# Routing logits of a mixture-of-experts kernel with the gate columns as TensorE weights, on four column groups

## The chip, the core and the metric

The kernel runs on one core of one Trainium2 chip. The metric is the device time of one execution in microseconds, the median of several. The profile is that of one execution; its span is what the hardware profiler recorded from the first to the last instruction. Engines are named as in the profile: PE is TensorE's products, PEld its weight loads, DVE VectorE, ACT ScalarE, POOL GpSimd, SP SyncE (which issues most DMAs).

## What is computed

Three layers stand one behind the other. Attention of 4 x 8 heads (576 positions, 64 wide) with a local or a strided mask gives `x` of 2304 tokens x 512. A dense feed-forward layer follows, then a mixture of 8 experts of which each token takes the one with the highest gate logit. The change touches the two products with `w_gate` and `w_output_gate`, 8 columns each.

```python
def _moe_ref(x, w_in, w_out):
    h = x @ w_in
    g = h * np.clip(h + 3.0, 0.0, 6.0) / 6.0
    return g @ w_out

def _moe2_ref(x, w_gate, w_output_gate, w1, w2):
    logits = x @ w_gate
    e_idx = np.argmax(logits, axis=1)
    ...
    eom = 1.0 / (1.0 + np.exp(-(x @ w_output_gate)))
    for e in range(E):
        mask = e_idx == e
        h = np.maximum(x[mask] @ w1[e], 0.0)
        out[mask] = gate_w[mask, None] * eom[mask, e, None] * (h @ w2[e])
```

## The kernel before

**Stages.** The 2304 tokens go in 6 chunks of 384 (three tiles of 128). Attention is cut into 32 groups, 0 to 31; its instructions are spread over the chunks ahead of the one that needs them: chunk 3 needs the groups up to 23, chunk 4 those up to 29, chunk 5 the last two. Behind chunk 5 come the experts (`A` and 1 to 7).

**A chunk's dense layer** has 16 steps f. A step has 12 products `h` (L542, 128x384, two PSUM buffers), ACT's `r` and `gh` (L546, L557), DVE's `r` and `gh` (L552, L564), then 9 products `x2` (L577, 128x512), which add up over f in three PSUM buffers, one for each tile.

**A group of attention** goes: scores `sa`, `sb` (L405, two row groups of 64) on PE; masks and minimum on DVE (L417); exponentials on ACT (L422); sum and reciprocal on DVE (L426, L427); `p` on POOL (L428); transpositions `ta`, `tb` (L452) on PE; their copy `pt` on ACT (L454); `o` (L469, 64-column groups) on PE; `xh` on ACT (L489) and `xl` on DVE (L490), which are the moving operands of `h`. On PE a group's transpositions stand ahead of the next group's scores, and `o` behind these.

**A chunk's routing** stands in the next chunk's first steps. The sums leave PSUM as `x2r` (`r_evac`: L592 on DVE for tiles 0 and 2, L590 on ACT for tile 1; three buffers); `r_trans` transposes them (`xt`, L603) and ACT copies the result to `x2T` (L608, one buffer). `r_logits` multiplies: in four products `x2T`'s 128 columns are the weights and `wgo`'s 16 columns (the two gates side by side) move; the result `lg` (L621) has a token in each partition. fp32 products are recorded as two instructions each. Then come `r_choose` and `r_rank` (`rk`, L651 to L655, weights `ones` and `tri`), and each tile's rows are scattered by POOL (L687) to the expert's place in `xs_d`. `sa`, `lg`, `rk` and `cntp` share one PSUM buffer ("s"); `sb`, `ta` and `xt` share another ("t").

**Chunk 5.** At step 7 `o_first` counts the tokens of each expert (`cntp`, L705); the first expert's number goes through a register to SP, which then issues the loads of its weights (L775) and, from step 10 on, of its rows and their numbers `e_m` (L826). DVE makes `e_i` of `e_m` (L854) and transposes the rows (L832).

**Order.** The code names an order in which work is handed on; within the loop over chunks a list scheduler then sets each engine's order by its own simulated times (attention with a higher priority), so a change in one place may move others. From the end of chunk 5 the order is written by hand.

Of the kernel before, what the change touches and what calls it, by code (L numbers as in the profile page):

```python
# [9 lines left out]
F32 = mybir.dt.float32  # L10
# [4 lines left out]
ACTF = mybir.ActivationFunctionType  # L15
ALU = mybir.AluOpType
AX = mybir.AxisListType
# [5 lines left out]
def kernel(  # L23
# [14 lines left out]
    nc = tc.nc  # L38
# [3 lines left out]
    E, _, DF2 = w1.shape  # L42
    KD = DM // 128
# [3 lines left out]
    NCH = NT // CH  # L47
# [3 lines left out]
    STR = 32  # L51
    NTB = S // STR
    SCL = 1.0 / float(D) ** 0.5
    NEG = -1.0e9 / SCL
    QB = 96
# [10 lines left out]
    const = ctx.enter_context(tc.tile_pool(name="const", bufs=1))  # L66
# [11 lines left out]
    ps_s = ph1.enter_context(tc.tile_pool(name="ps_s", bufs=1, space=PSUM))  # L78
# [4 lines left out]


    ident = const.tile([128, 128], F32, name="ident")
    mask_l0 = const.tile([QB, 128], F32, name="mask_l0")
    mask_l = const.tile([QB, 128], F32, name="mask_l")
    mask_s = const.tile([SB, SB], F32, name="mask_s")
    tri = const.tile([128, 128], F16, name="tri")
    ones = const.tile([128, 128], F16, name="ones")  # L90
    wgo = const.tile([128, KD, 2 * E], F32, name="wgo")
    three = const.tile([128, 1], F32, name="three")
    prio = const.tile([128, E], F32, name="prio")
    tok = const.tile([128, NTILE], F32, name="tok")
# [15 lines left out]

    def consts_attn():
        make_identity(nc, ident)
        for m, b0 in ((mask_l0, 0), (mask_l, STR)):

            nc.gpsimd.memset(m, 0.0)
            nc.gpsimd.affine_select(out=m, in_=m, pattern=[[-1, 128]], base=b0, channel_multiplier=1,
                                    compare_op=ALU.is_ge, fill=NEG)
            nc.gpsimd.affine_select(out=m, in_=m, pattern=[[1, 128]], base=STR - 1 - b0, channel_multiplier=-1,
                                    compare_op=ALU.is_ge, fill=NEG)
        ms = mask_s.rearrange("p (c j) -> p c j", c=CPB)  # L120
        nc.gpsimd.memset(mask_s, 0.0)
        for pat, base, cm in (([[-NTB, CPB], [-1, NTB]], 0, 1), ([[-NTB, CPB], [0, NTB]], 0, 1),
                              ([[NTB, CPB], [0, NTB]], NTB - 1, -1)):
            nc.gpsimd.affine_select(out=ms, in_=ms, pattern=pat, base=base, channel_multiplier=cm,
                                    compare_op=ALU.is_ge, fill=NEG)
        nc.gpsimd.memset(three, 3.0)

    def consts_route():
        nc.gpsimd.memset(tri, 1.0)
        nc.gpsimd.affine_select(out=tri, in_=tri, pattern=[[1, 128]], base=-1, channel_multiplier=-1,  # L130
                                compare_op=ALU.is_ge, fill=0.0)
        nc.gpsimd.iota(prio, pattern=[[-1, E]], base=E, channel_multiplier=0, allow_small_or_imprecise_dtypes=True)
        nc.gpsimd.iota(tok, pattern=[[128, NTILE]], base=-BIG, channel_multiplier=1,
                       allow_small_or_imprecise_dtypes=True)

        nc.gpsimd.memset(base16, 0.0)
        nc.gpsimd.iota(base16[0:1, :], pattern=[[NT, E]], base=0, channel_multiplier=0,
                       allow_small_or_imprecise_dtypes=True)
        nc.gpsimd.iota(eid, pattern=[[1, E]], base=0, channel_multiplier=0, allow_small_or_imprecise_dtypes=True)
        for p in range(E):  # L140
            nc.gpsimd.memset(capc[:, p:p + 1], float(CAPS[p]))
        nc.gpsimd.memset(acc[:, 0, :], 0.0)
        nc.sync.dma_start(out=wgo[:, :, 0:E], in_=w_gate.rearrange("(c p) e -> p c e", p=128))
        nc.sync.dma_start(out=wgo[:, :, E:2 * E], in_=w_ogate.rearrange("(c p) e -> p c e", p=128))

# [92 lines left out]
    def nat(u):  # L238

        return u < 2 * KD  # L240
# [137 lines left out]
    def blk(loc, i):  # L378
        if loc:
            k0 = 0 if i == 0 else QB * i - STR  # L380
            return QB * i, QB, k0, 128
        n = min(SB, S - SB * i)
        return SB * i, n, SB * i, n
# [3 lines left out]
    def banks(n, alt, a, b):  # L387

        pools = {"h": ps_h, "x2": ps_x, "s": ps_s, "t": ps_t}
        return [pools[tag].tile([128, 4, 128], F32, tag=tag, name=f"{nm}{n}") for tag, nm in (a, b)]  # L390

    def at_scores(n, alt=False):
        u, loc, bl = groups[n]
        qt, kt = qk_T["q", u], qk_T["k", u]
        if alt:
            s = banks(n, alt, *((("h", "sa"), ("h", "sb")) if n % 2 else (("s", "sa"), ("x2", "sb"))))
        else:
            s = banks(n, alt, ("s", "sa"), ("t", "sb"))

        with tc.manual_schedule(engines={mybir.EngineType.PE}):  # L400
            for j, i in enumerate(bl):
                q0, qn, k0, kn = blk(loc, i)
                for h2 in (1, 0):
                    p0 = 64 * h2
                    nc.tensor.matmul(s[h2][0:qn, j, 0:kn], lhsT=qt[p0:p0 + 64, q0:q0 + qn],  # L405
                                     rhs=kt[p0:p0 + 64, k0:k0 + kn], start=True, stop=True)
        if nat(u):
            w = w_p.tile([128, 2, 4, 128], F32, tag="w", name=f"p{n}")
            p = [w[:, h2] for h2 in range(2)]
        else:  # L410
            p = [a_p.tile([128, TPC, 128], F32, tag="p", name=f"p{n}_{h2}", bufs=2) for h2 in range(2)]
        st = a_p.tile([128, 2, 3, 4], F32, tag="st", name=f"st{n}", bufs=2)
        for h2 in range(2):
            for j, i in enumerate(bl):
                q0, qn, k0, kn = blk(loc, i)
                m = (mask_l0 if i == 0 else mask_l) if loc else mask_s
                nc.vector.tensor_tensor_reduce(  # L417
                    out=p[h2][0:qn, j, 0:kn], in0=s[h2][0:qn, j, 0:kn], in1=m[0:qn, 0:kn], scale=-SCL, scalar=3.0e38,
                    op0=ALU.add, op1=ALU.min, accum_out=st[0:qn, h2, 0, j:j + 1])
            for j, i in enumerate(bl):  # L420
                q0, qn, k0, kn = blk(loc, i)
                nc.scalar.activation(out=p[h2][0:qn, j, 0:kn], in_=p[h2][0:qn, j, 0:kn], func=ACTF.Exp,  # L422
                                     bias=st[0:qn, h2, 0, j:j + 1], scale=-1.0, accum_out=st[0:qn, h2, 1, j:j + 1])
            for j, c, qn, kn in runs(loc, bl):
                st1, st2 = (st[0:qn, h2, a, j:j + c] for a in (1, 2))
                nc.vector.tensor_scalar(out=st1, in0=st1, scalar1=1e-9, scalar2=None, op0=ALU.add)  # L426
                nc.vector.reciprocal(st2, st1)  # L427
                nc.gpsimd.tensor_tensor(out=p[h2][0:qn, j:j + c, 0:kn], in0=p[h2][0:qn, j:j + c, 0:kn],  # L428
                                        in1=st2.unsqueeze(2).to_broadcast([qn, c, kn]), op=ALU.mult)
        g_p_t[n] = p  # L430

    def runs(loc, bl):

        res = []
        for j, i in enumerate(bl):
            q0, qn, k0, kn = blk(loc, i)
            if res and res[-1][2:] == (qn, kn):
                res[-1] = (res[-1][0], res[-1][1] + 1, qn, kn)
            else:
                res.append((j, 1, qn, kn))  # L440
        return res
# [169 lines left out]
    def r_logits(c, t):  # L611

        if t == 0:
            rt[c] = (r_p.tile([128, 8, TPC, E], F32, tag="rt", name=f"rt{c}", bufs=1),
                     r_p.tile([128, 8, TPC], F32, tag="rm", name=f"rm{c}", bufs=1),
                     r_p.tile([128, TPC, E], F16, tag="oh", name=f"oh{c}", bufs=2),
                     r_p.tile([128, TPC], I32, tag="idx", name=f"idx{c}", bufs=2))
        o = x2T_t.pop((c, t))
        lg = ps_s.tile([128, 2 * E], F32, tag="s", name=f"lg{c}_{t}")
        for kt in range(KD):  # L620
            nc.tensor.matmul(lg, lhsT=o[:, kt, :], rhs=wgo[:, kt, :], start=(kt == 0), stop=(kt == KD - 1))  # L621
        nc.vector.tensor_copy(rt[c][0][:, 0:2, t, :], lg.rearrange("p (a e) -> p a e", a=2))

    def r_choose(c, a, z):
# [374 lines left out]
    for t in range(T0 + 1):  # L999
# [3 lines left out]
        if t == 1:  # L1003
            nc.tensor.matmul(warm[0:96, 0:256], lhsT=g_p_t[t][0][0:96, 0, 0:96],
                             rhs=ident[0:96].unsqueeze(1).to_broadcast([96, 2, 128]), start=True, stop=True)
# [82 lines left out]
    c = NCH - 1  # L1088
# [118 lines left out]
    with tc.If(total > 0):  # L1207
        with ExitStack() as ph3:
# [3 lines left out]
            with tc.For_i(0, E, 1) as e:  # L1212
# [5 lines left out]
                with tc.For_i(0, n_over, 128):  # L1218
# [20 lines left out]
                    for f in range(KF2):  # L1239
                        hp_ = ps_f.tile([128, 128], F32, name="hp_", bufs=2)  # L1240
                        for c in range(KD):
                            nc.tensor.matmul(hp_, lhsT=wr1[:, c, f * 128:(f + 1) * 128], rhs=xt[:, c, :],
                                             start=(c == 0), stop=(c == KD - 1))
                        nc.scalar.activation(out=ht[:, f, :], in_=hp_, func=ACTF.Relu)
                    yp = ps_f.tile([128, DM], F32, name="yp")
                    for f in range(KF2):
# [4 lines left out]
                        out=out, out_offset=bass.IndirectOffsetOnAxis(ap=ids.bitcast(U32), axis=0),  # L1251
                        in_=yr, in_offset=None, bounds_check=NT - 1, oob_is_err=False)
# [30 lines left out]
```

## Time and profile before

| | us |
|---|---|
| median of 3 runs | 867.54 (863.79 to 869.41) |
| profiled execution, its own time | 865.39 |
| its span | 863.6 |
| PE busy | 814.4 (94% of the span) |
| DVE, ACT, POOL busy | 469.7, 400.0, 112.7 |

The page's second part cuts the span into 40 slices of 21.6 us. PE is above 90% in nearly all of them from the ninth on; PEclk, the clock that TensorE was granted in tenths of 2.4 GHz, has a dip in one of them. No other engine reaches 60% over the span. The chain of waits that ended last names only the last scatter of the output, so that stages are read from the windows and from the timeline.

### The profile page before, as it was taken

How to read it: one execution, taken by the hardware profiler on the slowest of the kernel's cores; microseconds unless marked ns; L12 is line 12 of the kernel's file. 1: busy time of each engine (PE TensorE's matmuls, PEld its weight loads, DVE VectorE, ACT ScalarE, POOL GpSimd, SP SyncE). 2: the span in 40 equal slices, each digit the busy share in tenths (PEclk: the TensorE clock that was granted, in tenths of full speed). 3: DMA queues.
4: the chain of work that ended last, by engine and by line, in shares of the span. 5: the costliest groups of instructions: out<-in, count | busy, mean ns of one | idle time of the engine just before them, and what ended most of it. 6: DMA issues, size and time to landing. Idle time of an engine off the chain costs nothing. (4 is left out here: it accounts for less than half of the span.)

```text
span 863.6 us, 14576 instructions
## 1 busy us (share of the span) xinstructions
PE 814.4 (94%) x4928; PEld 692.7 (80%) x4929; DVE 469.7 (54%) x1412; ACT 400.0 (46%) x1054; POOL 112.7 (13%) x191
## 2 busy tenths in 40 slices
PE   7779989599999999999998999999999999999996
PEld 4555545257888888888877899988889999999995
DVE  3687446567764435453454232245656756766671
ACT  3785344467554334444344322334334544555551
POOL 3131003001200102110021010010100011011110
PEclk9669999699999999999997999999999999999999
DMA  3977216973212104320142010044066565657630
GB/s 92 288 218 223 89 51 114 198 171 65 69 34 41 33 9 79 76 42 20 28 109 40 1 39 1 1 134 124 38 190 197 162 183 174 185 180 214 190 127 19
DMA packets 179188, 91.68 MB, mean 106 GB/s; under 512 B 101369, under 2 KB 165113, under 8 KB 179112
## 3 DMA queue, kind: packets, MB, share of 16 engines
q1 hardware_dynamic: 175992, 81.15, 36.8%
q0 software_dynamic: 3120, 9.59, 2.9%
q8 instruction: 39, 0.64, 0.3%
q14 instruction: 37, 0.30, 0.1%
HBM read 74.63 MB, written 16.60 MB: 106 GB/s over the span
## 5 line engine op out<-in xcount | busy, mean ns | idle before, releaser
L577 PE MATMUL x<-wo,gh 128*128 128x512 f32 x720 | 188.3, 398 | 1.1 <-DVE gh L564 0.8
L542 PE MATMUL h<-xh,wi 128*128 128x384 f32 x640 | 182.1, 347 | 2.6 <-ACT xh L489 1.7
L577 PEld LDWEIGHTS x<-wo,gh 128*128 128x128 f32 x720 | 131.5, 188 | 26.5 <-DVE gh L564 2.2
L542 PEld LDWEIGHTS h<-xh,wi 128*128 128x128 f32 x640 | 119.0, 192 | 8.6 <-ACT xh L489 2.0
L546 ACT ACTIVATE r<-h,three 128x384 f32<-128x384 f32 x96 | 55.7, 580 | 133.9 <-PE h L542 76.8
L542 PE MATMUL h<-xl,wi 128*128 128x384 f32 x320 | 110.8, 346 | 0.6 <-DVE xl L490 0.6
L428 POOL TENSOR_TENSOR p<-p,st 126x126 f32<-126x126 f32 (+5 forms) x80 | 61.2, 782 | 366.5 <-DVE st L427 258.1
L552 DVE SCALAR_TENSOR_TENSOR r<-r,h 128x384 f32<-128x384 f32 x80 | 44.2, 552 | 109.0 <-ACT r L546 107.9
L422 ACT ACTIVATE p<-p,st 96x128 f32<-96x128 f32 (+2 forms) x176 | 67.1, 385 | 40.4 <-DVE st L417 40.4
L874 ACT ACTIVATE hh<-eh 128x128 fp32r<-128x128 f32 (+7 forms) x64 | 26.3, 411 | 102.2 <-PE eh L867 97.6
L875 DVE SCALAR_TENSOR_TENSOR hh<-eh,hh 128x128 fp32r<-128x128 f32 (+7 forms) x64 | 29.3, 458 | 74.6 <-ACT hh L874 67.2
L564 DVE TENSOR_TENSOR gh<-r,gh 128x384 fp32r<-128x384 f32 x80 | 46.4, 580 | 42.7 <-ACT gh L557 41.2
L557 ACT ACTIVATE gh<-r 128x384 fp32r<-128x384 f32 x80 | 42.0, 525 | 52.8 <-DVE r L552 43.1
L542 PEld LDWEIGHTS h<-xl,wi 128*128 128x128 f32 x320 | 61.5, 192 | 4.2 <-DVE xl L490 0.9
L572 PE MATMUL x<-wf,gh 128*128 128x512 f32 x96 | 47.2, 628 | 0.0
L538 PE MATMUL h<-x,wf 128*128 128x384 f32 x128 | 46.9, 512 | 0.2 <-DVE wf L215 0.2
L914 POOL DMA_INDIRECT out_dram<-yo,e_i x21 | 21.3, 1015 | 190.9 <-ACT yo L950 169.6
L405 PE MATMUL sb<-kT,qT 64*96 64x128 f32 (+2 forms) x176 | 33.6, 322 | 9.9 <-ACT pt L454 9.3
L538 PEld LDWEIGHTS h<-x,wf 128*128 128x128 f32 x128 | 24.9, 198 | 19.6 <-issue 6.0
L405 PEld LDWEIGHTS sb<-kT,qT 64*96 64x96 f32 (+2 forms) x176 | 24.6, 194 | 19.9 <-ACT pt L454 10.4
L687 POOL DMA_INDIRECT xs_d<-x2r,idx x18 | 19.0, 1054 | 161.8 <-DVE idx L658 110.8
L469 PE MATMUL o<-pt,v 128*64 128x96 f32 (+2 forms) x352 | 31.9, 293 | 2.3 <-ACT wo L221 1.5
(259 smaller groups left out, 1607.4 us busy)
## 6 DMA issues: line engine op xcount, KB each, us to landing
rawi<-in_moe_w_in_dram SPq DMA_DIRECT2D x16, 512.0 KB
rawo<-in_moe_w_out_dram SPq DMA_DIRECT2D x16, 512.0 KB
xs_d<-z SPq DMA_DIRECT2D x8, 792.0 KB
xs<-xs_d SPq DMA_DIRECT2D x28, 128.0 KB
qr<-in_q_dram SPq DMA_DIRECT2D x48, 72.0 KB
kr<-in_k_dram SPq DMA_DIRECT2D x48, 72.0 KB
v<-in_v_dram SPq DMA_DIRECT2D x20, 160.0 KB
er0i<-in_moe_w_dram SPq DMA_DIRECT2D x8, 256.0 KB
```

The costliest lines, as they stand in the source:

```text
L405: nc.tensor.matmul(s[h2][0:qn, j, 0:kn], lhsT=qt[p0:p0 + 64, q0:q0 + qn], rhs=kt[p0:p0 + 64, k0:k0 + kn], start=True, stop=True)
L422: nc.scalar.activation(out=p[h2][0:qn, j, 0:kn], in_=p[h2][0:qn, j, 0:kn], func=ACTF.Exp, bias=st[0:qn, h2, 0, j:j + 1], scale=-1.0, accum ...
L428: nc.gpsimd.tensor_tensor(out=p[h2][0:qn, j:j + c, 0:kn], in0=p[h2][0:qn, j:j + c, 0:kn], in1=st2.unsqueeze(2).to_broadcast([qn, c, kn]), ...
L469: nc.tensor.matmul(o[64 * h2:64 * h2 + 64, q0 - q00:q0 - q00 + qn], lhsT=vt[0:kn, i, :], rhs=pt[h2][0:kn, j, 0:qn], start=True, stop=True)
L538: nc.tensor.matmul(h, lhsT=w_val("i", f)[:, kt * 128:(kt + 1) * 128], rhs=x0[kt // 2][:, kt % 2], start=(kt == 0), stop=(kt == KD - 1))
L542: nc.tensor.matmul(h, lhsT=wa[f][:, a, kt, :], rhs=x[:, kt, c0:c0 + CH], start=(n == 0), stop=(n == 3 * KD - 1))
L546: nc.scalar.activation(out=r, in_=h, func=ACTF.Relu, bias=three, scale=1.0)
L552: nc.vector.scalar_tensor_tensor(out=r, in0=r, scalar=6.0, in1=h, op0=ALU.min, op1=ALU.mult)
L557: nc.scalar.activation(out=gh[:, 0, :], in_=r, func=ACTF.Copy)
L564: nc.vector.tensor_tensor(out=gh[:, 1, :], in0=r, in1=gh[:, 0, :].bitcast(F32), op=ALU.subtract)
L572: nc.tensor.matmul(acc_ps[c][t], lhsT=gh[:, t * 128:(t + 1) * 128], rhs=w_val("o", f), start=(f == 0), stop=(f == KF - 1))
L577: nc.tensor.matmul(acc_ps[c][t], lhsT=gh[:, g, t * 128:(t + 1) * 128], rhs=w[:, a, :], start=(f == 0 and n == 0), stop=(f == KF - 1 and n ...
```

## The change

For chunks 0 to 4 each of the four products of `r_logits` takes 32 columns of `wgo` as weights (16 gates and 16 zeros) and moves the 128 columns of `x2T`; each writes its own 32 partitions of a 128x128 tile `lp` and not one sum. ACT copies `lp` over `x2T`'s first part. One more product, with that copy as weights and a constant `sel_g` (16 columns, each with a one in four rows) moving, adds the four parts and turns them, so that `lg` comes out as before. Chunk 5 keeps the old products. Lines behind L618 move by 14 (`cntp` L705 becomes L719), those between by 3 (L542 becomes L545). The local mask is made once with 160 columns and read at an offset.

```diff
-    wgo = const.tile([128, KD, 2 * E], F32, name="wgo")
+    wgo = const.tile([128, KD, 32], F32, name="wgo")
+    sel_g = const.tile([128, 2 * E], F32, name="sel_g")
...
+        nc.gpsimd.memset(wgo, 0.0)
+        nc.vector.tensor_reduce(out=sel_g, in_=ident.rearrange("p (k e) -> p e k", k=KD)[:, 0:2 * E, :], axis=AX.X,
+                                op=ALU.add)
...
-                m = (mask_l0 if i == 0 else mask_l) if loc else mask_s
+                m = mask_l[:, STR if i == 0 else 0:] if loc else mask_s
...
         o = x2T_t.pop((c, t))
-        lg = ps_s.tile([128, 2 * E], F32, tag="s", name=f"lg{c}_{t}")
-        for kt in range(KD):
-            nc.tensor.matmul(lg, lhsT=o[:, kt, :], rhs=wgo[:, kt, :], start=(kt == 0), stop=(kt == KD - 1))
+        if c < NCH - 1:
+
+            lp = ps_s.tile([128, 128], F32, tag="s", name=f"lp{c}_{t}")
+            with tc.manual_schedule(engines={mybir.EngineType.PE}):
+                for kt in range(KD):
+                    nc.tensor.matmul(lp[32 * kt:32 * kt + 32, :], lhsT=wgo[:, kt, :], rhs=o[:, kt, :], start=True,
+                                     stop=True)
+            nc.scalar.activation(out=o[:, 0, :], in_=lp, func=ACTF.Copy)
+            lg = ps_s.tile([128, 2 * E], F32, tag="s", name=f"lg{c}_{t}")
+            nc.tensor.matmul(lg, lhsT=o[:, 0, :], rhs=sel_g, start=True, stop=True)
+        else:
+            lg = ps_s.tile([128, 2 * E], F32, tag="s", name=f"lg{c}_{t}")
+            for kt in range(KD):
+                nc.tensor.matmul(lg, lhsT=o[:, kt, :], rhs=wgo[:, kt, 0:2 * E], start=(kt == 0), stop=(kt == KD - 1))
```

The scheduler orders the whole program anew. Four places in which it now stands otherwise follow; a name's first numbers are group, or chunk and step (h3_0: chunk 3, step 0) or chunk and tile (x2_2_0).

**PE, from chunk 2 to chunk 3.** Before, behind group 23's output:

```order
L469 MATMUL o23_3584<-pt23_3481,v25_1_0_3268 64x96
L469 MATMUL o23_3584<-pt23_3481,v25_0_0_3133 64x96
L577 MATMUL x2_2_0_2929<-wo15_2618,gh2_15_3797 128x512 x3
L577 MATMUL x2_2_1_2930<-wo15_2618,gh2_15_3797 128x512 x3
L577 MATMUL x2_2_2_2931<-wo15_2618,gh2_15_3797 128x512 x3
L542 MATMUL h3_0_3809<-xh_116,wi0_1878 128x384
L542 MATMUL h3_1_3917<-xh_116,wi1_1896 128x384
```

and now:

```order
L472 MATMUL o23_3615<-pt23_3512,v25_1_0_3299 64x96
L472 MATMUL o23_3615<-pt23_3512,v25_0_0_3158 64x96
L545 MATMUL h3_0_3840<-xh_116,wi0_1873 128x384
L545 MATMUL h3_1_3948<-xh_116,wi1_1891 128x384
L545 MATMUL h3_0_3840<-xl_117,wi0_1873 128x384
```

Chunk 2's last nine `x2` products now stand ahead of group 23's transpositions; behind its output comes at once a product `h3_0` that reads it.

**PE, from chunk 3 to chunk 4.** Before, behind group 28's scores:

```order
L405 MATMUL sa28_4171<-kT12_4058,qT12_4056 96x128
L469 MATMUL o27_4313<-pt27_4152,v15_0_0_3532 64x126
L469 MATMUL o27_4313<-pt27_4152,v15_1_0_3649 64x72
L469 MATMUL o27_4313<-pt27_4152,v15_0_0_3532 64x72
L542 MATMUL h3_13_4671<-xh_116,wi13_2547 128x384
L542 MATMUL h3_13_4671<-xl_117,wi13_2547 128x384
L542 MATMUL h3_13_4671<-xh_116,wi13_2547 128x384 x2
L542 MATMUL h3_13_4671<-xl_117,wi13_2547 128x384
L542 MATMUL h3_13_4671<-xh_116,wi13_2547 128x384
L577 MATMUL x2_3_0_3942<-wo12_2453,gh3_12_4659 128x512 x3
```

and now:

```order
L408 MATMUL sa28_4220<-kT12_4095,qT12_4093 96x128
L472 MATMUL o27_4362<-pt27_4201,v15_1_0_3680 64x72
L472 MATMUL o27_4362<-pt27_4201,v15_0_0_3563 64x72
L580 MATMUL x2_3_0_3973<-wo15_2631,gh3_15_4792 128x512
L580 MATMUL x2_3_1_3974<-wo15_2631,gh3_15_4792 128x512
L580 MATMUL x2_3_2_3975<-wo15_2631,gh3_15_4792 128x512
L580 MATMUL x2_3_0_3973<-wo15_2631,gh3_15_4792 128x512 x2
L580 MATMUL x2_3_1_3974<-wo15_2631,gh3_15_4792 128x512 x2
L580 MATMUL x2_3_2_3975<-wo15_2631,gh3_15_4792 128x512 x2
L665 LDWEIGHTS ones_98
L665 MATMUL rk2_4323<-base16_114,ones_98 128x8
```

Half of step 13, steps 14 and 15 of `h` and `x2` of steps 12 to 14 have gone ahead of group 28's scores. Behind them are left the last `x2` of chunk 3, then chunk 2's rank products `rk2`, `ta28`, `tb28`, scores 29, `o28`, six `h4` products, `ta29`, `tb29`, scores 30, `o29`, and `h4_0`.

**DVE, at the same place.** Before, around the evacuation `x2r3_0`, which stands behind group 29's masks (L417):

```order
L417 ISA p29_1_4356,st29_4357<-sb29_4345,mask_l_96 96x128
L417 ISA st29_4357 96x1
L349 STREAM_TRANSPOSE qT28_4379<-qr28_4063 128x576
L349 STREAM_TRANSPOSE kT28_4381<-kr28_4068 128x576
L592 TENSOR_SCALAR x2r3_0_4782<-x2_3_0_3942 128x512
L490 TENSOR_TENSOR xl_117<-o28_4432,xh_116 128x288
```

and now:

```order
L671 TENSOR_REDUCE rm2_4005<-rt2_4004 128x3
L430 RECIPROCAL st28_4233<-st28_4233 96x3
L672 CAST idx2_4007<-rm2_4005 128x3
L595 TENSOR_SCALAR x2r3_0_4831<-x2_3_0_3973 128x512
L420 ISA p29_0_4404,st29_4406<-sa29_4393,mask_l_95 96x128
L420 ISA st29_4406 96x1
```

`x2r3_0` now stands ahead of group 29's masks, and right behind the indices `idx2` of chunk 2's scatters.

**PE in chunk 5, at `cntp`.** Before:

```order
L542 MATMUL h5_7_5638<-xl_117,wi7_2182 128x384
L542 MATMUL h5_7_5638<-xh_116,wi7_2182 128x384
L705 LDWEIGHTS ones_99
L705 MATMUL cntp_5666<-acc_104,ones_99 128x8
L542 MATMUL h5_8_5675<-xh_116,wi8_2221 128x384
L542 MATMUL h5_8_5675<-xl_117,wi8_2221 128x384
L542 MATMUL h5_8_5675<-xh_116,wi8_2221 128x384 x2
```

and now:

```order
L545 MATMUL h5_10_5837<-xl_117,wi10_2395 128x384
L545 MATMUL h5_10_5837<-xh_116,wi10_2395 128x384 x2
L719 LDWEIGHTS ones_98
L719 MATMUL cntp_5751<-acc_104,ones_98 128x8
L545 MATMUL h5_10_5837<-xl_117,wi10_2395 128x384
L545 MATMUL h5_10_5837<-xh_116,wi10_2395 128x384 x2
L545 MATMUL h5_10_5837<-xl_117,wi10_2395 128x384
```

`cntp` has moved from behind `h5_7` into `h5_10`: 31 products `h` and 27 products `x2` now stand ahead of it that stood behind it.

## Rows read from the trace of the kernel before

**Rows 1.** The page's first lines: busy time of the engines, and PE's clock in slices.

```profile
span 863.6 us, 14576 instructions
...
PE 814.4 (94%) x4928; PEld 692.7 (80%) x4929; DVE 469.7 (54%) x1412; ACT 400.0 (46%) x1054; POOL 112.7 (13%) x191
...
PEclk9669999699999999999997999999999999999999
```

**Rows 2.** Windows: us; PE, PEld, DVE, ACT, POOL busy (instructions); PEclk; DMA share; GB/s.

```profile
350.00:450.00 100.00, 100.00 (x620) 86.39 (x619) 47.55 (x186) 43.27 (x135) 13.57 (x29) 1.00 0.23 47
450.00:465.00 15.00, 11.57 (x57) 9.53 (x56) 6.84 (x29) 6.25 (x26) 3.22 (x4) 0.66 0.48 92
454.70:465.00 10.30, 8.41 (x41) 7.44 (x42) 3.64 (x20) 4.04 (x16) 1.76 (x3) 0.50 0.32 63
200.00:205.00 5.00, 5.00 (x29) 5.00 (x29) 3.24 (x8) 2.04 (x4) 2.73 (x2) 0.78 0.69 132
```

**Rows 3.** PE's timeline at a tile's logits: start, us, work, [idle before <-releaser].

```profile
203.12 0.96 PE L621 MATMUL lg<-wgo,x2T 128*128 128x16 f32 x8
203.93 0.63 PE L603 MATMUL xt<-ident,x2r 128*128 128x128 f32 x4
```

**Rows 4.** PE's timeline at group 29's scores, among `x2` products.

```profile
444.93 0.46 PE L405 MATMUL sb<-kT,qT 64*96 64x128 f32 x2
445.31 2.33 PE L577 MATMUL x<-wo,gh 128*128 128x512 f32 x9
...
447.76 0.27 PE L405 MATMUL sa<-kT,qT 64*96 64x128 f32 x1
...
447.87 0.27 PE L405 MATMUL sa<-kT,qT 64*96 64x128 f32 x1
...
448.40 0.72 PE L469 MATMUL o<-pt,v 128*64 128x96 f32 x12
```

**Rows 5.** Timeline of group 29's chain, from its last scores to chunk 4's first product.

```profile
448.09 0.38 PE L405 MATMUL sa<-kT,qT 64*96 64x128 f32 x2
...
454.12 0.47 PE L452 MATMUL ta<-ident,p 96*128 96x96 f32 x3 [0.84 <-POOL p L428]
...
454.62 0.41 ACT L454 ACTIVATE pt<-ta 128x288 f32<-128x288 f32 x1 [2.48 <-PE ta L452]
...
457.11 0.63 PE L405 MATMUL sa<-kT,qT 64*96 64x128 f32 x2
...
460.58 1.01 PE L542 MATMUL h<-xh,wi 128*128 128x384 f32 x2 [1.69 <-ACT xh L489]
```

**Rows 6.** Timeline of group 28: its last scores, and POOL's two halves of `p`.

```profile
433.52 0.38 PE L405 MATMUL sa<-kT,qT 64*96 64x128 f32 x2
...
437.61 1.61 POOL L428 TENSOR_TENSOR p<-p,st 96x384 f32<-96x384 f32 x2 [20.00 <-ACT r L546]
```

**Rows 7.** POOL's timeline: a scatter of chunk 2, and the next write to its buffer.

```profile
443.06 0.98 POOL L687 DMA_INDIRECT xs_d<-x2r,idx  x1 [0.30 <-issue]
...
445.94 0.11 POOL L594 MEMSET x2r<- 128x16 f32 x1 [0.31 <-DMA xs_d<-x2r,idx]
```

**Rows 8.** Timeline of chunk 5, PE and DVE, from `cntp` to `h5_15`.

```profile
570.56 0.18 PE L705 MATMUL cntp<-acc,ones 128*128 128x8 f16 x1
...
571.40 2.24 PE L577 MATMUL x<-wo,gh 128*128 128x512 f32 x9
573.48 0.33 PE L542 MATMUL h<-xl,wi 128*128 128x384 f32 x1
...
576.10 2.24 PE L577 MATMUL x<-wo,gh 128*128 128x512 f32 x9
...
585.60 0.17 DVE L854 TENSOR_SCALAR e_i<-e_m 128x2 int32<-128x2 f32 x1 [3.84 <-DMA e_m<-xs_d]
...
594.00 2.04 DVE L832 STREAM_TRANSPOSE xtA<-xsA 128x1024 f32<-128x1024 f32 x1
...
599.68 0.33 PE L542 MATMUL h<-xh,wi 128*128 128x384 f32 x1
```

More of the change, by code (lines that the diff above doesn't have):

```diff
@@ L85 @@
     ident = const.tile([128, 128], F32, name="ident")
-    mask_l0 = const.tile([QB, 128], F32, name="mask_l0")
-    mask_l = const.tile([QB, 128], F32, name="mask_l")
+    mask_l = const.tile([QB, 128 + STR], F32, name="mask_l")
     mask_s = const.tile([SB, SB], F32, name="mask_s")
@@ L112, in consts_attn @@
         make_identity(nc, ident)
[L113 to L119, printed above, removed]
+        nc.gpsimd.memset(mask_l, 0.0)
+        nc.gpsimd.affine_select(out=mask_l, in_=mask_l, pattern=[[-1, 128 + STR]], base=STR, channel_multiplier=1,
+                                compare_op=ALU.is_ge, fill=NEG)
+        nc.gpsimd.affine_select(out=mask_l, in_=mask_l, pattern=[[1, 128 + STR]], base=-1, channel_multiplier=-1,
+                                compare_op=ALU.is_ge, fill=NEG)
         ms = mask_s.rearrange("p (c j) -> p c j", c=CPB)
```

## The prediction

> **What bounds the kernel now.** I read the page's totals first: PE is busy 814.4 of 863.6 us, the next engine 469.7 [rows 1]. Then windows, since such a share is a mean over stages: from 350 to 450 us PE is busy 100.00 of 100 us at full clock, so there a product taken away shortens the run by its pitch, and an engine off the path counts only where PE comes to wait for it [rows 2]. Between 450 and 465, where chunk 3 gives way to chunk 4, PE is busy 11.57 of 15 us, and from 454.7 on the granted clock is 0.50, which is the lower of its two levels, 1.2 GHz [rows 2]. Last the timeline of that place: PE waits 0.84 us for POOL's `p` at group 29's transposition, and 1.69 us for the `xh` that ACT makes of its output [rows 5]. Only six scores, six outputs and some `h4` products were at hand to cover this chain. So two questions set the change's worth: what the products themselves save, and whether the new order still has work in front of each step of attention.
>
> The sum is made against the profiled execution, 865.39 us (span 863.6); that lies 2.15 below the median of 867.54, and I add this at the end. About 1% (8.7 us) is what a measurement of this kernel can tell from no change.
>
> **The products.** Before, a tile's eight instructions of `lg` take 0.81 us (203.12 to 203.93), 0.10 each [rows 3]. They are replaced by eight on four column groups and two of the old form. No row shows four column groups. The nearest are scores, which move 128 columns on two row groups: a lone visit of two instructions takes 0.38 us until the next `x2` starts (444.93 to 445.31), instructions in a row 0.11 each (447.76 to 447.87), `sa` beside `sb`; and `o`, on two column groups, runs 12 instructions of 96 columns in 0.72 [rows 4]. Groups thus overlap, and a visit costs 0.38 - 2 x 0.11 = 0.16 for going in and out. If all four overlap at no such price, `lp` takes 0.22; if they go one after another, 8 x 0.11 + 0.16 = 1.04. I take the lone visit and one pitch more for a start that is not quite together, 0.49, as it is nearest in form. With 2 x 0.10 for `lg` a tile takes 0.69 (0.42 to 1.24), and 15 tiles change by 15 x (0.69 - 0.81) = **-1.8** (-5.9 to +6.5).
>
> The visit's 0.16 agrees with the Trainium skill (TensorEngine Tiling (Array Packing), Tiling Modes), by which a change of tiling mode drains TensorE. The same page (Overview, Theoretical Speedup) gives up to four times the speed where a dimension is at most 32; an estimate by that is 0.81 / 4 = 0.20 for `lp`, 0.40 with `lg`, so -6.2 for the 15 tiles. The row of the lone visit speaks against it, which is why I don't take it.
>
> **ACT's copy** is 0.4 us for 288 columns [rows 5] and there are 15, on an engine at 46%. PE waits for it where nothing stands between `lp` and `lg`, and that is one tile (chunk 0's third); all others have over 2 us of `h` and `x2` between. The row to go by is `ta` to the end of `pt`, 454.12 to 455.03, 0.91 [rows 5]; less the products themselves I take **+0.6** (0.4 to 1.0). The set-up (a memset, a reduction, one mask fewer) stands on engines that wait for the first loads then: nothing; if that cover were gone, some tenths.
>
> **Chunk 2 to 3.** After the change 12 `o`, 15 `x2` and 6 `h` products are all that stand between the last scores of group 23 and its transposition. With pitches of 0.231 for `x2` (571.40 to 573.48, nine) and 0.175 for `h` (573.48 to 576.10, fifteen) [rows 8] and 0.06 for `o` that is 5.2 us; from the last scores of 29 to `ta` it took 6.0 (448.09 to 454.12) [rows 5]. PE would wait up to 0.8. Then `h3_0` stands right behind `o23`, and the nine `x2` products that covered this are gone. From `ta` to the first `h` took 454.12 to 460.58, 6.46 us, at the lower clock [rows 5]; PE's own part at full clock would make it some 5.3. Own work of transpositions, scores and outputs is about 1.6, so a wait of up to 3.7; the least is the 1.69 that ACT's `xh` alone cost [rows 5]. So 1.7 to 4.5; I take 3.2, the middle. Such waits have been followed by a lower clock: 0.78 from 200 to 205 us, that is 1.1 lost, and half of 10.3 at worst [rows 2]. Together **+4.3** (1.7 to 8).
>
> **Chunk 3 to 4.** Before, 433.52 [rows 6] to 460.58 [rows 5], 27.1 us, held 30 `h` and 27 `x2` products that now stand ahead of scores 28: 30 x 0.175 + 27 x 0.231 = 11.5. Without them, and with nothing else late, the stretch would be 15.6. But the chain through it can't shrink so: scores 28 to the first half of `p` 4.9 us (437.61 and half of 1.61) [rows 6], `ta` to the next group's last scores 3.0 (454.12 to 457.11), these to `ta29` 6.0, `ta29` to `h4_0` 6.46 [rows 5]: 20.4. That is 4.8 more. If groups 28 and 29 run at the best of these figures (4.9 also for the second, 5.3 for the end) it is 2.5. On DVE `x2r3_0` now stands ahead of group 29's masks and needs a buffer that a scatter of chunk 2 frees; a scatter took 2.9 us from issue to that (443.06 to 445.94) [rows 7]. Scores 29 come some 8 us behind scores 28 in any case, so most of it is covered: +1.0 (0 to 2.9). Together **+5.8** (2.5 to 7.7).
>
> **Chunk 5.** `cntp` comes 31 x 0.175 + 27 x 0.231 = 11.7 us later in PE's order. Behind it are queued the register, SP's loads of the first expert and `e_m`, whose landing DVE already waited 3.84 us for, at 585.60 [rows 8]. If all of it moves, `e_m` is there at 597.3, where DVE's order now has `e_i` and the transposition L832 (2.04 [rows 8]) ahead of `gh5_12`, two splits and `r5_13`, about 5.8 in all; `h5_15`, which needs the buffer that `r5_13` frees, would start at 603.1 and not at 599.68 [rows 8]: +3.4. The loads behind `cntp` may have waited for buffers rather than for the count, in which case nothing is lost. I take half, **+1.7** (0 to 3.4).
>
> Sum: -1.8 + 0.6 + 4.3 + 5.8 + 1.7 = +10.6, so 876.0 on the profiled scale and **878.1** on that of the median.
>
> **The rivals.** *The chains are better covered than I count.* ACT, DVE and POOL have room, and a group with nothing else in its engines' queues may run faster than 29 did beside chunk 3's last step. With half of the terms at both boundaries and none in chunk 5: -1.8 + 0.6 + 2.2 + 2.9 = +3.9, 871.4; with none of them, 866.3. Against it: groups 28 and 29 in the trace already made PE wait with more work in front of them.
>
> *The change doesn't do what it says:* the four column groups take their turns, since each has weights of its own to load. Then the products cost +6.5 in place of -1.8, and the time is 886. For it speaks that no row shows more than two groups at once; against it `o`, whose two column groups do overlap at 0.06 each.
>
> *Faster than before:* the four groups overlap fully, going in and out costs nothing, and no boundary waits: -5.9 + 0.6 = -5.3, or 862. It decides at group 28: PE has o27's products and nine `x2`, some 2.5 us, in front of `ta28`, so scores must become `p` in less than that; 4.9 were measured. The Trainium skill's factor of four (TensorEngine Tiling (Array Packing), Overview) would give the same price of the products, and its drain (Tiling Modes) speaks against it.
>
> **How the numbers follow.** The forecast, with waits at both boundaries, has 0.62 and lies between 872 and 886; about 0.16 of it lies below 876.2, where slower by 1% begins. Better covered chains: 0.18, all within 1%. Groups in turn: 0.08, slower. Full overlap and no waits: 0.07, of which 0.03 below 858.9. Anything else 0.05: 0.01 faster, 0.01 the same, 0.03 slower. So slower 0.46 + 0.08 + 0.03 = 0.57, the same 0.16 + 0.18 + 0.04 + 0.01 = 0.39, faster 0.04. The range 867 to 888 leaves out the fastest case, a little of the covered one, half of the groups in turn, and most of the rest, about 0.16.
>
> **What the profile after would show.** The products: `lp` near 0.5 us a tile from its first instruction to what follows; near 0.2 or 1.0 the rivals have it. Boundaries: rows of PE with idle time of 1 us and more ahead of `h3_0`, `ta28`, `ta29` and `h4_0`, ended by ACT's `xh` or POOL's `p`, and a second slice of PEclk below 9 near chunk 3's start. Chunk 5: DVE's wait ahead of `e_i` ends near 597 and `h5_15` starts some 3 us late by chunk 5's own time. The forecast is wrong if PE stays busy through the start of chunk 3, or if a wait of several us stands at a place that I haven't named, above all in chunks 0 to 2, whose order moved as well.

## The result and the profile after

The changed kernel takes 877.83 us (median of 4 runs, 875.96 to 880.0), the kernel before 866.02 beside it (4 runs): the ratio is 1.0146, 95% interval 1.0107 to 1.0185, so 11.8 us more. The forecast was 878.1. The profiled execution after is one of 880.0 us, 14.6 above the one of before, which is 2.8 more than the medians differ by; single executions of either kernel spread by as much. Of the 14.6, 3.3 lie ahead of the routing's first transposition `xt` (199.21 against 195.88 us), where no new product has run yet; that stretch scatters as much between the traces of this case (194.60 in run 1, 200.24 in run 5).

The page's first lines after, which answer to [rows 1]:

```profile
span 878.0 us, 14647 instructions
...
PE 816.3 (93%) x4958; PEld 688.5 (78%) x4959; DVE 470.1 (54%) x1413; ACT 403.0 (46%) x1069; POOL 110.4 (13%) x189
...
PEclk9568999698999999999986999999999999999998
```

PE is as busy as before, so the span's growth is waiting: the totals already say that no engine got much more to do. The windows of after tell where, against [rows 2] (us; PE, PEld, DVE, ACT, POOL busy; PEclk; DMA share; GB/s):

```profile
350.00:450.00 100.00, 97.87 (x600) 83.84 (x596) 45.51 (x172) 43.45 (x133) 12.70 (x25) 1.00 0.23 47
450.00:480.00 30.00, 23.21 (x142) 19.07 (x141) 13.92 (x66) 12.95 (x51) 8.72 (x15) 0.66 0.49 106
...
600.00:620.00 20.00, 16.15 (x74) 14.13 (x73) 14.10 (x23) 10.63 (x21) 0.00 (x0) 0.91 0.80 205
```

Three stretches hold waits: the start of chunk 3 (in the first window), the start of chunk 4, and chunk 5's last steps.

**The products.** PE's timeline of after at a tile of chunk 0, against [rows 3]:

```profile
207.44 0.33 PE L545 MATMUL h<-xh,wi 128*128 128x384 f32 x1
207.70 0.43 PE L627 MATMUL lp<-x2T,wgo 128*32 128x128 f32 x8
208.06 0.66 PE L606 MATMUL xt<-ident,x2r 128*128 128x128 f32 x4
208.47 0.42 PE L545 MATMUL h<-xh,wi 128*128 128x384 f32 x1
208.73 0.34 PE L545 MATMUL h<-xl,wi 128*128 128x384 f32 x1
...
212.76 0.29 PE L631 MATMUL lg<-sel_g,x2T 128*128 128x16 f32 x2
212.90 0.42 PE L545 MATMUL h<-xh,wi 128*128 128x384 f32 x1
213.16 0.34 PE L545 MATMUL h<-xl,wi 128*128 128x384 f32 x1
```

and of before, behind the `xt` of [rows 3]:

```profile
204.32 0.42 PE L542 MATMUL h<-xh,wi 128*128 128x384 f32 x1
204.58 0.33 PE L542 MATMUL h<-xl,wi 128*128 128x384 f32 x1
```

A pitch is the time from one start to the next. Eight instructions of `lp` take 0.36 us up to the next work, the last `h` ahead of them has a pitch of 0.26 where 0.17 is usual, and `xt` behind them takes 0.41 and not 0.39: 0.47 in all. `lg` takes 0.14, but the `h` behind it has a pitch of 0.26 too, which is 0.09 more. Before, a tile had one such slow `h` on the way out, behind `xt` (204.32 to 204.58); now it has two (208.47 to 208.73, 212.90 to 213.16), since `lg` is a visit by itself. A tile so costs 0.47 + 0.14 + 0.09 = 0.70 and not 0.81, which is 0.11 less, and 1.7 us less for 15 tiles. The one tile whose `lg` stands right behind `lp`:

```profile
229.24 0.43 PE L627 MATMUL lp<-x2T,wgo 128*32 128x128 f32 x8
230.12 0.39 PE L631 MATMUL lg<-sel_g,x2T 128*128 128x16 f32 x2 [0.46 <-ACT x2T L629]
```

**Chunk 2 to 3.** PE's timeline of after:

```profile
366.63 0.51 PE L545 MATMUL h<-xh,wi 128*128 128x384 f32 x2
368.06 1.64 PE L580 MATMUL x<-wo,gh 128*128 128x512 f32 x6 [0.92 <-DVE gh L567]
...
372.34 0.72 PE L472 MATMUL o<-pt,v 128*64 128x96 f32 x12
374.10 0.62 PE L545 MATMUL h<-xh,wi 128*128 128x384 f32 x2 [1.05 <-ACT xh L492]
```

PE waits where the order lacks work: chunk 2's last `x2` stand right behind the step that makes their `gh`, and `h3_0` right behind `o23`. `ta23` waits for nothing. The clock stays at 1.00.

**Chunk 3 to 4.** Timeline of after (PE, POOL and DVE), against [rows 5 to 7]:

```profile
451.37 0.38 PE L408 MATMUL sa<-kT,qT 64*96 64x128 f32 x2
...
455.44 1.61 POOL L431 TENSOR_TENSOR p<-p,st 96x384 f32<-96x384 f32 x2 [27.21 <-DVE st L430]
456.32 0.55 PE L455 MATMUL ta<-ident,p 96*128 96x96 f32 x3 [1.74 <-POOL p L431]
...
459.31 0.63 PE L408 MATMUL sa<-kT,qT 64*96 64x128 f32 x2
...
460.63 0.69 DVE L595 TENSOR_SCALAR x2r<-x 128x512 f32<-128x512 f32 x1 [5.08 <-DMA xs_d<-x2r,idx]
...
464.20 1.01 PE L545 MATMUL h<-xh,wi 128*128 128x384 f32 x2 [3.11 <-ACT xh L492]
...
466.43 0.68 PE L455 MATMUL ta<-ident,p 96*128 96x96 f32 x3
...
472.60 1.01 PE L545 MATMUL h<-xh,wi 128*128 128x384 f32 x2 [1.69 <-ACT xh L492]
```

From group 28's last scores (451.37) to `h4_0` (472.60) it is 21.2 us; 20.4 and 1.0 were forecast. Its parts: 4.95 to `ta28`, 2.99 to the last scores of 29, 7.12 to `ta29`, 6.17 to `h4_0`. `x2r3_0` does hold DVE for the scatter, until 460.63, and group 29's masks behind it start at 461.23, 1.92 us behind its last scores; before it was 0.52 (448.09 to 448.61).

**Chunk 5.** Timeline of before (PE), the one wait of `x2` there:

```profile
586.67 1.66 PE L577 MATMUL x<-wo,gh 128*128 128x512 f32 x6 [0.82 <-DVE gh L564]
```

and of after (PE and DVE), against [rows 8]:

```profile
593.55 0.18 PE L719 MATMUL cntp<-acc,ones 128*128 128x8 f16 x1
...
608.60 0.17 DVE L868 TENSOR_SCALAR e_i<-e_m 128x2 int32<-128x2 f32 x1 [3.88 <-DMA e_m<-xs_d]
608.81 1.99 DVE L846 STREAM_TRANSPOSE xtA<-xsA 128x1024 f32<-128x1024 f32 x1
...
611.29 0.73 PE L580 MATMUL x<-wo,gh 128*128 128x512 f32 x2 [1.71 <-DVE gh L567]
...
614.16 0.69 PE L545 MATMUL h<-xh,wi 128*128 128x384 f32 x1 [2.14 <-DVE r L555]
```

From `cntp` to `e_i` it is 15.05 us, before 15.04 (570.56 to 585.60): all of the delay is handed on. DVE reaches `gh5_12` and `r5_13` late, and PE waits 1.71 and 2.14; behind the second wait it has the lower clock for some 3 us (0.50 from 614 to 617).

### The profile page after: what moved, and what is told of

It reads as the page before. It is cut to its first block, busy times and chain, and to the rows that moved or that the text cites. A ratio compares the mean times of both kernels' runs of the same rounds, so it can differ in the third digit from the quotient of the medians.

```text
span 878.0 us, 14647 instructions
## 1 busy us (share of the span) xinstructions
PE 816.3 (93%) x4958; PEld 688.5 (78%) x4959; DVE 470.1 (54%) x1413; ACT 403.0 (46%) x1069; POOL 110.4 (13%) x189
## 3 DMA queue, kind: packets, MB, share of 16 engines
q1 hardware_dynamic: 175992, 81.15, 37.7%
## 5 line engine op out<-in xcount | busy, mean ns | idle before, releaser
L580 PE MATMUL x<-wo,gh 128*128 128x512 f32 x720 | 190.3, 399 | 2.6 <-DVE gh L567 2.6
L545 PE MATMUL h<-xh,wi 128*128 128x384 f32 x640 | 184.1, 351 | 8.7 <-ACT xh L492 5.8
L545 PEld LDWEIGHTS h<-xh,wi 128*128 128x128 f32 x640 | 120.6, 194 | 15.3 <-ACT xh L492 6.6
L545 PE MATMUL h<-xl,wi 128*128 128x384 f32 x320 | 112.1, 350 | 0.0
L545 PEld LDWEIGHTS h<-xl,wi 128*128 128x128 f32 x320 | 62.4, 195 | 4.2 <-issue 0.9
L408 PEld LDWEIGHTS sb<-kT,qT 64*96 64x96 f32 (+2 forms) x176 | 24.2, 190 | 20.4 <-ACT pt L457 11.6
```

The costliest lines, as they stand in the source:

```text
L545: nc.tensor.matmul(h, lhsT=wa[f][:, a, kt, :], rhs=x[:, kt, c0:c0 + CH], start=(n == 0), stop=(n == 3 * KD - 1))
L580: nc.tensor.matmul(acc_ps[c][t], lhsT=gh[:, g, t * 128:(t + 1) * 128], rhs=w[:, a, :], start=(f == 0 and n == 0), stop=(f == KF - 1 and n ...
```

## The experiments

The theory: the products themselves save some 2 us, and the order that comes with them loses more at the three places. Where the texts on record put the saving at 0.22 us a tile (0.59 for 0.81), they leave out the way out of `lg`; the comparisons below take 0.11. The rival: the new logits cost the time where they stand. Every ratio is against the kernel before on the same chip; us are the ratio times that kernel's median there (862.4, 864.2, 866.9 and 865.0 us for runs 1 to 4, 5 to 8, 9 to 11, and 12).

**One place at a time.** The order of the three places depends on different chunks' logits, so that each loss can be had alone. The edit of run 1; runs 2, 3 and 4 have `c < 2`, `c == 2` and `c == 4` there:

```diff
-        if c < NCH - 1:
+        if c in (0, 3):
```

Run 1, chunks 0 and 3 (none of the three places):

> The new logits in chunks 0 and 3 alone, the old ones in 1, 2 and 4. PE's order at the starts of chunks 3 and 4 and at cntp is then as before. By the theory that the time is lost through the order at these three places: 6 tiles at 0.59 and not 0.81 us, -1.3, and the one wait of 0.46 for ACT's copy in chunk 0, so -0.9 us against before, ratio 0.999. By the rival that the new logits cost the time where they stand (11.8 us over 15 tiles, 0.8 each): +4.7 us, ratio 1.0055.

Measured: 1.0042 (1.0018 to 1.0066), +3.6 us. By the time alone the rival's +4.7 is nearer than the theory (-0.2 with 0.11 a tile), so that the rows must decide: the trace has no wait at the starts of chunks 3 and 4 that before lacks, but one of 1.80 in chunk 5 (0.82 before), with the clock at 0.50 from 586.7 to 590.1 behind it. These are worth 2.7. Such a wait needs no new logits: in runs 2, 3, 5, 9 and 12, where `cntp` stands as before, it is 1.03 to 1.67. About 1 us was left over, and more in the next three runs.

Run 2, chunks 0 and 1 (start of chunk 3):

> The new logits in chunks 0 and 1 alone. Only the start of chunk 3 is ordered as in the changed kernel (4.8 us of work ahead of ta23, none between o23 and h3_0). By the order: -1.3 for the products, +0.5 for the copy's wait, and the two waits of 0.9 and 1.0 us at the start of chunk 3 with what they bring behind them, together +1 to +3 us, ratio 1.001 to 1.0035, and the waits ahead of chunk 4 as before. By the rival: +4.7 us, as with chunks 0 and 3.

Measured: 1.0065 (1.0046 to 1.0084), +5.6 us. The waits are those of the changed kernel, 0.92 and 1.05 at chunk 3 and 0.46 for the copy, and no others are new; with 0.7 for the products they give 1.7, some 4 us less than was measured.

Run 3, chunk 2 (start of chunk 4):

> The new logits in chunk 2 alone. Only the start of chunk 4 is ordered as in the changed kernel (2.5 us of work ahead of ta28, 1.3 ahead of ta29). By the order: PE waits of about 1.7, 3.1 and 1.7 us ahead of ta28 and h4_0 and the lower clock for 20 us and not 10, 5.6 us, less 0.7 for the products: +4.9 us, ratio 1.0057. By the rival that three tiles cost 0.8 each: +2.4 us, and nothing at chunk 4's start.

Measured: 1.0094 (1.0058 to 1.0130), +8.1 us. PE's timeline of run 3 has waits at the same three products, but the middle one is not the expected 3.1:

```profile
444.91 0.38 PE L408 MATMUL sa<-kT,qT 64*96 64x128 f32 x2
...
449.87 0.47 PE L455 MATMUL ta<-ident,p 96*128 96x96 f32 x3 [1.73 <-POOL p L431]
...
456.13 1.01 PE L545 MATMUL h<-xh,wi 128*128 128x384 f32 x2 [1.69 <-ACT xh L492]
...
465.34 1.01 PE L545 MATMUL h<-xh,wi 128*128 128x384 f32 x2 [1.69 <-ACT xh L492]
```

Here `x2r3_0` stands behind group 29's masks on DVE (456.06 against 454.70), and ahead of them in the changed kernel. From group 28's last scores to `h4_0` it is 20.4 us and not 21.2, so that the hold for the scatter is worth about 0.8. By 20.4 - 15.6, less 0.3 for the products, run 3 should lose 4.5; 3.6 were left over.

Run 4, chunk 4 (`cntp`):

> The new logits in chunk 4 alone. Only cntp stands later on PE, by 31 products h and 27 products x2. By the order: DVE gets e_m some 11 us later, with a wait of PE ahead of h5_15, +3.9 us, less 0.7: +3.2 us, ratio 1.0037; PE's waits ahead of chunk 4 as before. By the rival that three tiles cost 0.8 each: +2.4 us, lost in the first five steps of chunk 5 and not at its end. By a second rival, that the count was not what SP waited for: -0.7 us.

Measured: 1.0057 (1.0036 to 1.0077), +4.9 us. Run 4's timeline of PE, and of DVE:

```profile
597.40 0.73 PE L580 MATMUL x<-wo,gh 128*128 128x512 f32 x2 [1.54 <-DVE gh L567]
600.27 0.69 PE L545 MATMUL h<-xh,wi 128*128 128x384 f32 x1 [2.14 <-DVE r L555]
```

```profile
594.69 0.17 DVE L868 TENSOR_SCALAR e_i<-e_m 128x2 int32<-128x2 f32 x1 [3.57 <-DMA e_m<-xs_d]
```

`cntp` stands at 579.82, 9.3 later than before, `e_i` comes at 594.69, 9.1 later, and the two waits are at `gh5_12` and `r5_13`: the count is what SP waits for, and the second rival falls. Less 0.3 for the products the waits give 3.3; 1.6 were left over. Each loss came at its place and only with its chunk; the rival of evenly spread costs has no wait to show, and runs 3 and 4 lose more than its +2.4. But all four runs were above their sums, by 1 to 4 us, and what they share is the set-up.

**The set-up.** Run 5 keeps it and takes all new logits away:

```diff
-        if c < NCH - 1:
+        if c < 0:
```

> The change without its logits: all chunks keep the old products, but the merged mask, the wider wgo with its memset and sel_g are there; PE's order is that of before. Runs 1 to 4 came out 3 to 5 us above what their products and waits give. If the set-up is what they share: about +3 us, ratio 1.0035, and PE late already by the first steps of chunk 1. If the set-up costs nothing, as was predicted: ratio 1.000, and the surplus belongs to the new logits.

Measured: 1.0025 (1.0000 to 1.0049), +2.2 us. So there was a cost where none had been forecast, but its interval touches 1. The change's constants are 64 bytes shorter in all, so that every later tile in SBUF begins 64 bytes lower. Run 9 gives the 64 bytes back (first edit, in run 5), run 12 puts 64 bytes into the kernel before (second edit, alone):

```diff
-    sel_g = const.tile([128, 2 * E], F32, name="sel_g")
+    sel_g = const.tile([128, 4 * E], F32, name="sel_g")[:, 0:2 * E]
...
-    three = const.tile([128, 1], F32, name="three")
+    three = const.tile([128, 17], F32, name="three")[:, 0:1]
```

> Run 5 with sel_g's tile made 64 bytes longer, nothing else. The change's constants are 64 bytes shorter in all than before, so that in run 5 and in the changed kernel every later tile in SBUF begins 64 bytes lower than before; with these 64 bytes they begin where they did. If the addresses are what the set-up costs: ratio 1.000, about 2 us below run 5. If it is the memset, the reduction or the merged mask, or chance: as run 5, 1.0025.

> The kernel before with one constant's tile 64 bytes longer and nothing else: every engine's order is that of before, and every later tile in SBUF begins 64 bytes higher. If addresses off by 64 bytes are what runs 1 to 5, 7, 8 and 11 share: ratio 1.002 to 1.003, the hardware queue's transfers 324 to 334 us of 16 engines' time for the same packets, and SP's 41st transfer issued after 30.8 us. If it was the set-up's work, or chance: ratio 1.000, 318 to 323 us, and 30.1 to 30.7.

Measured: run 9 0.9986 (0.9963 to 1.0008), run 12 1.0021 (1.0002 to 1.0039), +1.8 us. The window from 30 to 60 us, first of before, then of run 9:

```profile
30.00:60.00 30.00, 22.43 (x184) 18.08 (x182) 25.84 (x107) 26.59 (x96) 9.47 (x11) 0.67 0.80 238
```

```profile
30.00:60.00 30.00, 22.50 (x183) 18.18 (x182) 25.72 (x108) 26.78 (x96) 8.96 (x11) 0.67 0.80 238
```

and then of run 5 and of run 12:

```profile
30.00:60.00 30.00, 22.50 (x170) 17.70 (x170) 23.24 (x101) 24.79 (x94) 7.67 (x10) 0.61 0.90 238
```

```profile
30.00:60.00 30.00, 24.72 (x179) 19.86 (x180) 25.55 (x107) 26.41 (x96) 8.94 (x11) 0.56 0.86 238
```

The last two columns are the point: at the same 238 GB/s the DMA engines are busy 0.80 of the time at the old addresses, and 0.90 and 0.86 when they are off by 64 bytes. Over a whole run, the hardware queue's 175992 packets (81.15 MB) keep the 16 engines busy 36.8% of the span in before and 37.1% in run 9, but 38.3% and 38.0% in runs 5 and 12. All 14 traces of the case part by it, though narrowly: 318 to 323 us in the four with the old addresses, 324 to 334 in the ten with others. They part more clearly by the window from 30 to 60 us (0.78 to 0.80 against 0.86 to 0.91) and by what waits for the weights there: ACT's waits for `rawi`, the weights that `_moe_ref` calls `w_in`, add up to 11.3 to 12.5 us in the first 200 us of the four and to 13.1 to 15.6 in those of the ten. Run 12's third sign decides nothing: SP's 41st transfer was issued at 30.76, between the two cases.

**Where the order comes from.** `lp` and `lg` share the "s" buffer with attention's scores `sa` and transpositions `tb`. In the changed kernel each tile holds it twice, ACT's copy and mostly some 4 us of other products lie between, and the `lp` of chunk 4 come 9.6 us apart (560.05, 569.67, 579.17) where `lg` came 5.9 apart (548.31, 554.20, 560.04). Runs 6 to 8 put the logits of chunks 0 to 4 into `h`'s two buffers and change nothing else in the order's making: run 6 in the kernel before (first edit), run 7 in the changed one (second edit, and `lg` alike).

```diff
-        lg = ps_s.tile([128, 2 * E], F32, tag="s", name=f"lg{c}_{t}")
+        lg = (ps_h if c < NCH - 1 else ps_s).tile([128, 2 * E], F32, tag="h" if c < NCH - 1 else "s", name=f"lg{c}_{t}")
...
-            lp = ps_s.tile([128, 128], F32, tag="s", name=f"lp{c}_{t}")
+            lp = ps_h.tile([128, 128], F32, tag="h", name=f"lp{c}_{t}")
```

> The kernel before, with lg of chunks 0 to 4 in one of the two PSUM buffers of h and not in the one buffer that it shares with attention's scores. The order then has 8.4 us of work ahead of ta29 and 15.9 between o29 and h4_0, and cntp where it was. By the order theory: PE's waits of 0.84 and 1.69 us ahead of chunk 4 and the stretch at the lower clock behind them go, -3 to -6 us, ratio 0.993 to 0.9965. If h's buffers are missed: PE waits ahead of h in the steps that hold logits, 15 times some tenths, and the gain is gone.

> The changed kernel with lp and lg both in h's buffers. Work ahead of ta23, ta28 and ta29 8.4, 6.5 and 7.6 us, 8.9 ahead of h3_0 and 17.4 ahead of h4_0, cntp where it was before the change. By the order theory: none of the three losses, the products' 3.3 us kept, so 3 us faster than run 6, plus what run 5 shows of the set-up: against before 0.990 to 0.998, and 12 us and more below the changed kernel. If the new logits themselves were the loss: about as slow as the changed kernel, 1.01.

Measured: run 6 0.9981 (0.9962 to 1.0001), -1.6 us; run 7 1.0029 (1.0009 to 1.0048), +2.5 us, the old addresses being off in it too. The window over chunk 4's start, in run 6 and in run 7:

```profile
430.00:480.00 50.00, 50.00 (x304) 43.41 (x304) 18.39 (x60) 20.26 (x56) 4.87 (x10) 1.00 0.10 18
```

```profile
430.00:480.00 50.00, 50.00 (x293) 42.77 (x292) 21.59 (x71) 22.03 (x67) 5.33 (x10) 1.00 0.15 28
```

Neither has a wait left there, nor the lower clock, and the changed kernel's waits at chunks 3 and 5 are gone in run 7. But some of it is given back at chunk 0's logits, at 220 to 230 us: run 6 waits 0.52, 0.64 and 0.82, its clock 0.86 from 220 to 232; run 7 has this:

```profile
226.97 0.46 PE L408 MATMUL sb<-kT,qT 64*96 64x128 f32 x2 [2.55 <-ACT x2T L611]
227.36 0.43 PE L627 MATMUL lp<-x2T,wgo 128*32 128x128 f32 x8
228.65 0.61 PE L631 MATMUL lg<-sel_g,x2T 128*128 128x16 f32 x2 [0.86 <-ACT x2T L629]
```

So run 7's -3 us and more against run 6 did not come: it is 4.1 us above it. The addresses are about 2 of that; these waits, and the clock of 0.57 from 228 to 236 us behind them, are worth the rest and what the products save.

Run 8 takes the four column groups out of run 7:

```diff
-                    nc.tensor.matmul(lp[32 * kt:32 * kt + 32, :], lhsT=wgo[:, kt, :], rhs=o[:, kt, :], start=True,
-                                     stop=True)
+                    nc.tensor.matmul(lp[0:32, :], lhsT=wgo[:, kt, :], rhs=o[:, kt, :], start=(kt == 0),
+                                     stop=(kt == KD - 1))
...
-            nc.tensor.matmul(lg, lhsT=o[:, 0, :], rhs=sel_g, start=True, stop=True)
+            nc.tensor.matmul(lg, lhsT=o[0:32, 0, :], rhs=ident[0:32, 0:2 * E], start=True, stop=True)
```

> As run 7, but the four products of lp add up in the first 32 partitions, all on one column group, and the turning product takes these 32 rows alone. If the four groups do run beside each other (0.36 us for eight instructions), one group takes 8 x 0.11 = 0.86, and the kernel is 15 x 0.5 = 7 us slower than run 7. If it is the 32 columns as weights and not the four groups that made lp short: as run 7.

Measured: 1.0165 (1.0124 to 1.0206), 11.0 us above run 7. PE's timeline of run 8:

```profile
495.38 1.06 PE L627 MATMUL lp<-x2T,wgo 128*32 128x128 f32 x8
496.37 2.33 PE L580 MATMUL x<-wo,gh 128*128 128x512 f32 x9
498.64 0.39 PE L631 MATMUL lg<-ident,x2T 32*128 32x16 f32 x2
498.96 0.44 PE L545 MATMUL h<-xh,wi 128*128 128x384 f32 x1
```

One group takes 0.99 for the eight, four take 0.36: they do run beside each other. The turning product over 32 rows takes 0.32 where that over 128 took 0.14. Both together are 0.81 a tile, 12.2 us. In chunk 0 run 8 has one wait of 4.36 for the copy (224.35) in place of run 7's 2.55 and 0.86.

**All together.** Runs 10 and 11 keep the old logits in chunk 0 and have the new ones in chunks 1 to 4, all in `h`'s buffers; run 10 has the 64 bytes of run 9 too. The edit beside run 7's:

```diff
-        if c < NCH - 1:
+        if 0 < c < NCH - 1:
...
-            lg = ps_s.tile([128, 2 * E], F32, tag="s", name=f"lg{c}_{t}")
+            p_lg, t_lg = (ps_h, "h") if c < NCH - 1 else (ps_s, "s")
+            lg = p_lg.tile([128, 2 * E], F32, tag=t_lg, name=f"lg{c}_{t}")
```

> Old logits in chunk 0, new ones in chunks 1 to 4, all with their PSUM tiles in h's buffers, and sel_g's tile 64 bytes longer. Run 7's waits of 2.6 and 0.9 us behind chunk 0's third tile can't arise. By the order theory: run 6 less 12 tiles at 0.22 us, -1.6 - 2.6 = -4.2 us against before, ratio 0.995, if the addresses are the set-up's cost, 0.9975 if not. If the new logits cost as much as they save: 0.998 as run 6.

> As run 10 without the 64 bytes. If the addresses are the set-up's cost: 2 us slower than run 10. If not: as run 10.

Measured: run 10 0.9970 (0.9949 to 0.9992), -2.6 us; run 11 0.9996 (0.9971 to 1.0021), 2.0 us above run 10 by medians, as the addresses give. Run 10 beats both kernels, and the rival's 0.8 us a tile, 9.4 for its twelve tiles, is not there. Its advance over run 6 is 1 us where twelve tiles give 1.4 at 0.11, not the 2.6 of its text; the two were on different chips, and the intervals don't settle how much of the products' gain is left in it.

## Why the prediction was right

The forecast of 878.1 was met (877.83), and the side and the mechanism hold: a cheaper product, and an order that leaves chains of attention and the count uncovered. That the two times lie 0.3 apart is luck: the forecast began at 867.54, the median of four runs of before is 866.02, and 10.6 us were forecast where 11.8 were measured. By its terms, in the order of the sum:

- **The products**, -1.8 forecast, -1.7 by the rows: 0.69 a tile was forecast and 0.70 measured. `lp` was put at 0.49 (measured 0.47: a lone visit and one pitch) and `lg` at 0.20 (0.14, and 0.09 for the way out, which the forecast didn't name). The bound at which the groups take their turns is what run 8 shows for one group.
- **ACT's copy**, +0.6 forecast, 0.46 at the one tile.
- **Chunk 2 to 3**, +4.3 forecast, 2.1 by the window from 350 to 450. The chain from transposition to output was taken from group 29 at the lower clock, and put at 5.3 at full clock; `ta23` to `h3_0` was 3.9 us (370.24 to 374.10). The wait of up to 0.8 ahead of `ta23` and the fall of the clock did not come. Not named: `x2` waiting 0.92 for `gh`.
- **Chunk 3 to 4**, +5.8 forecast, 21.2 - 15.6 = 5.6. Its parts hold too: 20.4 for the chain alone, as in run 3, and 0.8 for the scatter where 1.0 was put. Of the places named for a wait, `ta29` has none; the `h4` products ahead of it wait 3.11.
- **Chunk 5**, +1.7 forecast, 3.9 by the rows. The step that failed is the halving: of the two cases put there, the count or the buffers, it is the count, and all of it is handed on (15.05 against 15.04 us). For that case the forecast had worked out 3.4; by chunk 5's own time `h5_15` starts 3.2 us late, 20.6 us behind `cntp` where 29.1 less the 11.7 that moved are 17.4. The 3.9 are the two waits alone; the 0.82 that PE waited there before and the lower clock behind them (some 3 us, so about 1.5 lost) stand against each other and are left out.
- **The set-up**, 0 forecast, about +2 (runs 5, 9 and 12). What covers the memset and the reduction was named rightly, and they cost nothing that run 9 shows (0.9986, 0.9963 to 1.0008); the addresses were not thought of.

The sum by measured terms is -1.7 + 0.5 + 2.1 + 5.6 + 3.9 + 2 = 12.4, against 11.8 (9.3 to 16.0). Three terms were off by about 2 us, chunk 2 to 3 one way, chunk 5 and the set-up the other, and two of these errors cancel. Of the rivals, better covered chains fell in runs 2 to 4, groups in turn in run 8, and the fast case at `ta28`, which waited 1.74 us as its condition said.

In the part of the Trainium skill that was weighed (TensorEngine Tiling (Array Packing), Overview), up to four times the speed gave an estimate of 0.20 for `lp`. The trace has 0.45 with the way in and 0.36 without it; eight instructions on one group against four groups, 0.99 to 0.36, are 2.8 times. The measurement decides.

## What to carry to other kernels

Where a scheduler orders the program, an edit in the routing is also an edit of everything that shares its buffers: read in the new order how much work stands between a producer and its consumer at each boundary, and price that from the chain in the old trace. A product that becomes two with a copy between holds a shared buffer twice; here another buffer for both was worth 10 us (1.0146 against 1.0029, run 7), and the products' own time 1.7. Price a product with its way in and its way out: one visit that becomes two pays them twice. And keep the addresses when constants change size, or measure the size alone.

## What was not expected of the hardware

Tiles that begin 64 bytes off cost a kernel with 81 MB of transfers 1.8 us (run 12, 1.0002 to 1.0039, same instructions in the same order): between 30 and 60 us the DMA engines are busy 0.86 and not 0.80 of the time for the same 238 GB/s. Which transfers suffer was not tried. A turning product over 32 of the 128 rows took longer than one over all 128: 0.32 us (run 8) against 0.14 up to the next product, for two instructions of 16 columns among full-size ones. And the two instructions of `lg`, 0.14 themselves, slow the next `h` from 0.17 to 0.26.
